# Two attention blocks on one core: A's Exps three tiles behind their projections, other orders at the first transposes and the last out-projections

## The chip, the core and the metric

The kernel runs on one core of a Trainium2 chip. Its engines work side by side, each on its own queue in order: TensorE (PE in the profile, its weight loads PEld) multiplies matrices into PSUM, ScalarE (ACT) computes Exp and copies, VectorE (DVE) does elementwise work and copies, GpSimd (POOL) makes a few constants, SyncE (SP) issues DMAs. An engine waits on semaphores that the others raise. The metric is the device time of one execution in microseconds (us); lower is better. Before the change the median of three runs is 1082.8 us (1082.65 to 1332.74).

## The reference

Two attention blocks work on separate inputs of shape 1 x 2048 x 512, with 32 heads of 16 channels, and their outputs stand side by side in the last dimension.

```python
# A: linear attention                         # B: softmax attention
qkv = x @ wqkv ; q, k, v per head             qkv = x @ wqkv ; q, k, v per head
phi(t) = where(t > 0, t + 1, exp(t)) + 1e-6   p = softmax(q @ k.T * 16 ** -0.5)
pq, pk = phi(q), phi(k)                       o = p @ v
o = (pq @ (pk.T @ v)) / (pq . sum(pk) + 1e-6)
out_a = o @ wo                                out_b = o @ wo
```

## The kernel before

**Block B is the backbone.** Its scores are cut into blocks of 128 keys by 512 queries. A unit is one of two heads in each of four pairs (four heads at once, in four row groups of the array) for one chunk of 512 queries: 64 blocks. There are 32 units, 2048 blocks, and a tile is three blocks, so 683 tiles. For tile s, `QK(s)` (L453) is three matmuls into one of two PSUM buffers pS of three banks each, `EXP(s)` (L462) is one ScalarE Exp over 128 x 1536 from pS into one of NP = 8 SBUF buffers PT, and `PV` (L469) is one matmul a block into pPV, where a unit accumulates. At the end of a unit VectorE copies pPV to OT (L475), and `unit_norm` transposes and divides (L484 to L490).

**The order is written by a loop over steps s.** A step emits what `later` has put at this step, then `EXP(s)`, `QK(s + 2)`, up to six `PV`s of tiles before s, and then at most one misc job (`issue_misc`). QK(s + 2) needs the PSUM buffer that EXP(s) reads. Each engine runs its own instructions in the order in which they were emitted.

**Misc jobs** are all other work: B's remaining projections (`proj`, `vproj`), block A as a whole, norms and out-projections. They share one PSUM bank, MISC (pM). Each job has a hold, the number of steps until the next one may be issued. Block A's are, in order: transposes of x (L356), then for each of 16 row tiles `a_k` (L536, four matmuls of 512 columns, hold 4) and `a_v` (L544, the same size, hold 2), four `a_kv`, then in four rounds four `a_q` (L563, four matmuls of 512 columns, hold 4), a denominator, and four times numerator, transpose (`out_tr`, L501/L504) and out-projection (`out_mm`, L511/L514, four matmuls of 512 columns, then a store to DRAM).

**phi.** `a_k` and `a_q` end in `phi`: ScalarE takes an Exp of pM into EA (L526), VectorE clamps EA (L527) and combines (L529). `later(1, st1)` puts these three one step after the projection, so that in ScalarE's queue EA's Exp stands right ahead of EXP(s + 1). There are 32 of them.

**Start and end.** Ahead of the loop PE warms up with 14 small matmuls (L604), four pairs of row tiles of x are transposed into six borrowed pS banks, and the first projections run. After the loop the last unit's four row tiles go one after the other through out_tr and out_mm in the bank MISC, with VectorE alone copying out. Then `bound_end` (L395 to L403) reduces bounds on the scores to one number FLG. Every engine loads FLG and branches (L737, L738): above a threshold a general, slower softmax would run. With these inputs it does not.

Of the kernel before, what the change touches and what calls it, by code (L numbers as in the profile page):

```python
# [19 lines left out]
class Sched:  # L20
# [75 lines left out]

    def emit_queue(self, queue, eng, sems, dma_inc=16):
        waited = {}
        for op in self.queue_ops[queue]:
            for d in op.waits:  # L100
                is_dma = d.lane not in self.ENGINES
                val = d.count * (dma_inc if is_dma else 1)
                if waited.get(d.lane, 0) >= val:
                    continue
                eng.wait_ge(sems[d.lane], val)
                waited[d.lane] = val
            ins = op.fn(eng)
# [105 lines left out]
def bass_concat_heads__linear_attn_block__softmax_full_mha__prompt_kernel(nc, A_x, A_wqkv, A_wo, B_x, B_wqkv, B_wo, out):  # L213
# [8 lines left out]
    TB = 3  # L222
    NP = 8
    NBLK = NU * NT * 4
# [4 lines left out]
    with es:  # L229
# [24 lines left out]
        ZR = sb("ZR", [128, 2, 16], F32)  # L254
        ONT = sb("ONT", [128, 2, 512], BF)
        OB = sb("OB", [128, 4, 512], BF)
        OA = sb("OA", [128, 2, 512], BF)
# [108 lines left out]
        def proj(bk, Gp, sc, kind, lane="dve"):  # L366
# [8 lines left out]
            if kind == 0:  # L375
                ev("dve", bk, lambda e, bk: e.tensor_copy(QT[:, r, cs], f32v(bk)), [], [("QT", r, sc)])
            else:
                for e_ in range(2):
                    ev("dve", bk, lambda e, bk, e_=e_: e.tensor_scalar(KM[:, r, e_, cs], f32v(bk), PAR[:, e_:e_ + 1], None, op0=ALU.mult),  # L379
                       [("PAR", e_)], [("KM", r, e_, sc)])  # L380
# [113 lines left out]

        out_lanes = {"a": [sch.new_dma_lane() for _ in range(2)], "b": [sch.new_dma_lane() for _ in range(2)]}
        stores = []
# [10 lines left out]
        def out_mm(bk, ab, t, o2, lane="dve"):  # L507
            WO, wkey, col0, o4 = (WOa, "WOa", 0, o2) if ab == "a" else (WOb, "WOb", 512, 2 + o2)
            def mm(e, bk):
                for hb in range(4):  # L510
                    ins = e.matmul(f32v(bk), lhsT=ONT[:, o2, hb * 128:(hb + 1) * 128], rhs=WO[:, hb, :], start=(hb == 0), stop=(hb == 3))  # L511
                return ins
            pe(bk, mm, [("ONT", o2), wkey])
            ev(lane, bk, lambda e, bk: (e.tensor_copy(OB[:, o4, :], f32v(bk)) if lane == "dve"  # L514
                                        else e.activation(OB[:, o4, :], f32v(bk), ACTF.Copy)), [], [("OB", o4)])
            stores.append(sch.add(out_lanes[ab][o2], lambda e: e.dma_start(out[0][t * 128:(t + 1) * 128, col0:col0 + 512], OB[:, o4, :]),
                                  reads=[("OB", o4)], queue="sp", force_signal=True))

# [3 lines left out]
        def phi(bk, out_ap, okeys):  # L522
            q = ectr[0] % 2
            ectr[0] += 1
            def st1():
# [76 lines left out]
        def warm(e):  # L602
            for i_ in range(14):
                ins = e.matmul(MB[:, 0:128], lhsT=identb[:], rhs=identb[:], start=True, stop=True)  # L604
            return ins
        sch.add("pe", warm, reads=["identb"], writes=["MB"])
        xb_in = lambda t: on_keys(t) + on_keys(t + 1)
        xT(SBANKS[0], ON, xb_in(0), xTb, "xTb", 0, lane="dve")
        xT(SBANKS[1], ON, xb_in(2), xTb, "xTb", 2, lane="act")
        proj(SBANKS[2], 0, 0, 1)  # L610
        proj(SBANKS[3], 0, 0, 0)
        xT(SBANKS[4], ON, xb_in(4), xTb, "xTb", 4, lane="act")
        xT(SBANKS[5], ON, xb_in(6), xTb, "xTb", 6, lane="dve")
# [17 lines left out]
        for Gp in range(1, NGP):  # L631
# [4 lines left out]
            for sc in range(NC):  # L636
                for kind in (1, 0):
                    bproj.append((r0, 3, lambda bk, Gp=Gp, sc=sc, kind=kind: (proj(bk, Gp, sc, kind), later(2, lambda: bound(Gp, sc, kind)))))
        aj = []
        for t in range(0, NT, 2):  # L640
            aj.append((0, 2, lambda bk, t=t: xT(bk, KNa, [("KNa", t), ("KNa", t + 1)], xTa, "xTa", t)))
        for t in range(NT):
            aj.append((0, 4, lambda bk, t=t: a_k(bk, t)))
            aj.append((0, 2, lambda bk, t=t: a_v(bk, t)))
        for bq in range(4):
            aj.append((0, 3, lambda bk, bq=bq: a_kv(bk, bq)))
        for sc in range(NC):
            for bq in range(4):
                aj.append((0, 4, lambda bk, sc=sc, bq=bq: a_q(bk, sc, bq)))
            aj.append((0, 3, lambda bk, sc=sc: a_den(bk, sc)))  # L650
# [17 lines left out]
        def unit_done(u, s):  # L668
# [4 lines left out]
            if Gp == NGP - 1 and e_ == 1:  # L673
                for tl in range(4):
                    t = 4 * c + tl
                    outb_q.append((s + 4, 2, lambda bk, t=t: out_tr(bk, ON[:, t, :], on_keys(t), t % 2)))
                    outb_q.append((s + 4, 2, lambda bk, t=t: out_mm(bk, "b", t, t % 2)))

        QK(0)
        QK(1)  # L680
        npv = 0
# [3 lines left out]
        while True:  # L685
# [26 lines left out]
            if s >= NTILE and npv == NBLK and not (norm_q or early or bproj or outb_q or aj) and not at_step:  # L712
                break
        bound_end(MISC)

        last = {}
# [17 lines left out]
        def run(queue, e):  # L734
            sch.emit_queue(queue, e, sems)
            e.wait_ge(sems["dve"], flag_op.count)
            v = e.value_load(FLG.bitcast(mybir.dt.int32)[0:1, 0:1], min_val=0)  # L737
            with e.If(v > THRESHOLD_BITS):  # L738
                for ln, tot in totals.items():
# [52 lines left out]
```

## Time and profile before

The profiled execution took 1080.88 us, its span, from the first to the last instruction, is 1079.2 us.

| | before |
|---|---|
| median of three runs | 1082.8 us |
| profiled execution | 1080.88 us |
| its span | 1079.2 us |
| ScalarE busy | 942.0 us, 87% of the span |
| PE busy | 827.3 us, 77% |
| VectorE busy | 225.4 us, 21% |
| mean granted clock of TensorE | 0.749 of full speed |

ScalarE is busiest. A busy PE need not be at its peak, since matmuls overlap. The granted clock of a stretch is a mean over its two levels, 1.0 (2.4 GHz) and 0.5 (1.2 GHz).

### The profile page before, as it was taken

The numbers are of one execution on the slowest core, as the hardware profiler recorded it, in microseconds if no ns is written. First come the engines' busy times: TensorE is split into PE (matmuls) and PEld (weight loads), VectorE is DVE, ScalarE is ACT, GpSimd is POOL, SyncE is SP. The second block draws the span as 40 slices with busy tenths as digits, with TensorE's granted clock in tenths as the row PEclk, the third lists the DMA queues.
The fourth block names the chain that finished last, engine by engine and source line by source line (L and its number), as shares of the span: only waits on it lengthen the run. The fifth ranks groups of instructions, "written<-read, shape, count | busy, mean of one in ns | idle before, by whom it ended". The sixth has DMA issues, their size and how long they took to land.

```text
span 1079.2 us, 11753 instructions
## 1 busy us (share of the span) xinstructions
PE 827.3 (77%) x5212; PEld 227.0 (21%) x5264; DVE 225.4 (21%) x395; ACT 942.0 (87%) x719; POOL 4.9 (0%) x16
## 2 busy tenths in 40 slices
PE   6877777776777776876886877687888887888875
PEld 3322221111111221221221222122111112121211
DVE  3532431111211331121221234112000002010202
ACT  5999998767877997897887999789999999999990
POOL 1000000000000000000000000000000000000000
PEclk9999997677776996596676689658655558585865
DMA  9000000000000000000000000000000000000000
GB/s 310 2 1 1 1 1 1 0 1 1 1 1 0 1 1 1 1 15 5 5 15 1 5 6 5 6 1 15 5 1 1 1 1 20 1 20 1 16 5 22
DMA packets 13128, 13.39 MB, mean 12 GB/s; under 512 B 1808, under 2 KB 12560, under 8 KB 13072
## 3 DMA queue, kind: packets, MB, share of 16 engines
q1 hardware_dynamic: 12272, 12.19, 3.5%
q8 instruction: 42, 0.69, 0.3%
q10 hardware_dynamic: 800, 0.39, 0.1%
q14 instruction: 14, 0.11, 0.0%
HBM read 8.39 MB, written 4.19 MB: 12 GB/s over the span
## 4 chain that ended last, share of the span: by engine, by line
ACT 73%; PE 23%; DVE 1%; issue 1%; DMA 0%
ACT PT L462 71%; PE pS L453 6%; PE pPV L469 6%; PE pM L544 2%; PE pM L511 2%; PE pM L563 2%; ACT EA L526 2%; PE pM L536 1%; PE pM L484 1%; PE pM L501 1%; DMA ON<-in_B_x_dram 0%; PE pS L369 0%; PE pM L369 0%; PE pS L356 0%; DVE KM L379 0%
## 5 line engine op out<-in xcount | busy, mean ns | idle before, releaser
L462 ACT ACTIVATE PT<-pS 128x1536 bf16<-128x1536 f32 (+1 forms) x683 | 922.6, 1591 | 13.7 <-PE pS L453 12.8
L453 PE MATMUL pS<-QT,KM 32*128 32x512 bf16 x2048 | 338.6, 490 | 219.7 <-ACT PT L462 218.3
L469 PE MATMUL pPV<-PT,VV 128*17 128x512 bf16 x2048 | 333.6, 488 | 1.3 <-DVE VV L426 0.9
L453 PEld LDWEIGHTS pS<-QT,KM 32*128 32x128 bf16 x2048 | 69.0, 95 | 496.3 <-ACT PT L462 473.0
L469 PEld LDWEIGHTS pPV<-PT,VV 128*17 128x17 bf16 x2048 | 62.3, 89 | 214.7 <-issue 210.4
L526 ACT ACTIVATE EA<-pM 128x512 bf16<-128x512 f32 x32 | 19.1, 597 | 89.1 <-PE pM L563 45.8
L475 DVE COPY OT<-pPV 128x512 f32<-128x512 f32 x32 | 22.1, 691 | 236.1 <-PE pPV L469 236.0
L514 DVE CAST OB<-pM 128x512 bf16<-128x512 f32 x32 | 22.1, 692 | 89.5 <-PE pM L511 89.5
L527 DVE TENSOR_SCALAR EA<-EA 128x512 bf16<-128x512 bf16 x32 | 9.4, 294 | 113.9 <-ACT EA L526 113.9
L369 PE MATMUL pM<-xTb,Wb 128*128 128x512 bf16 x108 | 29.2, 390 | 3.3 <-DVE xTb L363 1.7
L547 DVE CAST VNa<-pM 128x512 bf16<-128x512 f32 x16 | 11.1, 694 | 98.7 <-PE pM L544 98.7
L484 PE MATMUL pM<-identf,OT 128*128 128x128 f32 x128 | 29.3, 370 | 1.3 <-DVE OT L475 1.3
L379 DVE TENSOR_SCALAR KM<-pM,PAR 128x512 bf16<-128x512 f32 x30 | 21.1, 746 | 35.5 <-PE pM L369 35.5
L544 PE MATMUL pM<-Wa,xTa 128*128 128x512 bf16 x58 | 26.3, 601 | 1.9 <-issue 1.9
L504 DVE COPY ONT<-pM 128x512 bf16<-128x512 bf16 x32 | 13.6, 425 | 57.7 <-PE pM L501 57.7
L563 PE MATMUL pM<-xTa,Wa 128*128 128x512 bf16 x57 | 22.4, 531 | 1.6 <-issue 1.6
L511 PE MATMUL pM<-WOb,ONT 128*128 128x512 bf16 x57 | 20.4, 490 | 3.8 <-DVE ONT L504 2.5
L488 DVE RECIPROCAL ZR<-pM 128x16 f32<-128x16 f32 x32 | 8.2, 257 | 70.0 <-PE pM L484 70.0
L484 PEld LDWEIGHTS pM<-identf,OT 128*128 128x128 f32 x128 | 18.7, 184 | 15.8 <-issue 7.9
L511 PE MATMUL pM<-WOa,ONT 128*128 128x512 bf16 x50 | 19.6, 496 | 2.7 <-issue 2.6
L390 DVE TENSOR_REDUCE KMX<-KM 128x1 f32<-128x1024 bf16 x16 | 19.5, 1217 | 0.4
L590 DVE TENSOR_TENSOR OA<-pM,RD 128x512 bf16<-128x512 f32 x16 | 11.1, 691 | 25.0 <-PE pM L586 25.0
(76 smaller groups left out, 253.9 us busy)
## 6 DMA issues: line engine op xcount, KB each, us to landing
out_dram<-OB SPq DMA_DIRECT2D x32, 128.0 KB, 1.7
KNa<-in_A_x_dram SPq DMA_DIRECT2D x4, 512.0 KB, 8.3
ON<-in_B_x_dram SPq DMA_DIRECT2D x3, 512.0 KB, 7.7
Wa<-in_A_wqkv_dram SPq DMA_DIRECT2D x1, 1536.0 KB, 12.6
Wb<-in_B_wqkv_dram SPq DMA_DIRECT2D x2, 384.0 KB, 8.4
Wb<-in_B_wqkv_dram SPq DMA_DIRECT2D x1, 512.0 KB, 6.8
WOb<-in_B_wo_dram SPq DMA_DIRECT2D x1, 512.0 KB, 12.7
WOa<-in_A_wo_dram SPq DMA_DIRECT2D x1, 512.0 KB, 12.5
```

The lines of the kernel that those rows point to most:

```text
L369: ins = e.matmul(f32v(bk), lhsT=Wb[:, cc, kind * 512 + Gp * 128:kind * 512 + Gp * 128 + 128], rhs=xTb[:, cc, sc * 512:(sc + 1) * 512], sta ...
L379: ev("dve", bk, lambda e, bk, e_=e_: e.tensor_scalar(KM[:, r, e_, cs], f32v(bk), PAR[:, e_:e_ + 1], None, op0=ALU.mult), [("PAR", e_)], [( ...
L453: ins = e.matmul(SCR[b][:, i * 512:(i + 1) * 512], lhsT=KM[32 * g:32 * g + 32, Gp % 2, e_, j * 128:(j + 1) * 128], rhs=QT[32 * g:32 * g + ...
L462: sch.add("act", lambda e: e.activation(PT[:, t % NP, 0:w], SCR[b][:, 0:w], ACTF.Exp, scale=SC), reads=skeys(b), writes=[("PT", t % NP)], ...
L469: sch.add("pe", lambda e: e.matmul(PVb[32 * g:32 * g + 17, 0:512], lhsT=VV[:, j, 17 * h:17 * h + 17], rhs=PT[:, t % NP, i * 512:(i + 1) * ...
L475: sch.add("dve", lambda e: e.tensor_copy(OT[:, u % 2, :], PVb[:, 0:512]), reads=[("PV", g) for g in range(4)], writes=[("OT", u % 2)])
L484: ins = e.transpose(f32v(bk)[:, qb * 128:(qb + 1) * 128], OT[:, ob, qb * 128:(qb + 1) * 128], identf[:])
L511: ins = e.matmul(f32v(bk), lhsT=ONT[:, o2, hb * 128:(hb + 1) * 128], rhs=WO[:, hb, :], start=(hb == 0), stop=(hb == 3))
L514: ev(lane, bk, lambda e, bk: (e.tensor_copy(OB[:, o4, :], f32v(bk)) if lane == "dve" else e.activation(OB[:, o4, :], f32v(bk), ACTF.Copy)) ...
L526: ev("act", bk, lambda e, bk: e.activation(EA[:, q, :], f32v(bk), ACTF.Exp), [], [("EA", q)])
L544: ins = e.matmul(f32v(bk), lhsT=xTa[:, cc, t * 128:(t + 1) * 128], rhs=Wa[:, cc, 1024:1536], start=(cc == 0), stop=(cc == 3))
L563: ins = e.matmul(f32v(bk), lhsT=Wa[:, cc, bq * 128:(bq + 1) * 128], rhs=xTa[:, cc, sc * 512:(sc + 1) * 512], start=(cc == 0), stop=(cc == 3))
```

## The change

The Exps of phi move from one step after the projection to three, and `a_k` and `a_q` hold MISC for five steps, not four. The first transposes take one row tile each, copied out alternately by VectorE and ScalarE; QK(0) and QK(1) come earlier, and two transposes and a projection behind them; the warm-up is 28 matmuls, not 14. When all tiles are through, the last four transposes and then the last four out-projections go over the six pS banks, copied out alternately by ScalarE and VectorE, with more ONT and OB buffers and six store lanes. `bound_end` becomes a misc job behind B's last projection; a hook has each engine load FLG in mid-queue, so that only the branch stays at the end. NP becomes 7.

```diff
@@ emit_queue
+            if hook is not None and op.idx > hook[0]:
+                hook[1](eng)
+                hook = None
             ins = op.fn(eng)
@@
-    NP = 8
+    NP = 7
@@
-        ONT = sb("ONT", [128, 2, 512], BF)
-        OB = sb("OB", [128, 4, 512], BF)
+        ONT = sb("ONT", [128, 6, 512], BF)
+        OB = sb("OB", [128, 6, 512], BF)
@@ proj
             if kind == 0:
-                ev("dve", bk, lambda e, bk: e.tensor_copy(QT[:, r, cs], f32v(bk)), [], [("QT", r, sc)])
+                ev(lane, bk, lambda e, bk: (e.tensor_copy(QT[:, r, cs], f32v(bk)) if lane == "dve"
+                                            else e.activation(QT[:, r, cs], f32v(bk), ACTF.Copy)), [], [("QT", r, sc)])
@@ phi
-            later(1, st1)
+            later(3, st1)
@@ the start
-            for i_ in range(14):
+            for i_ in range(28):
...
-        xT(SBANKS[0], ON, xb_in(0), xTb, "xTb", 0, lane="dve")
-        xT(SBANKS[1], ON, xb_in(2), xTb, "xTb", 2, lane="act")
-        proj(SBANKS[2], 0, 0, 1)
-        proj(SBANKS[3], 0, 0, 0)
-        xT(SBANKS[4], ON, xb_in(4), xTb, "xTb", 4, lane="act")
-        xT(SBANKS[5], ON, xb_in(6), xTb, "xTb", 6, lane="dve")
+        for t in range(4):
+            xT(SBANKS[t], ON, on_keys(t), xTb, "xTb", t, n=1, lane=("dve", "act")[t % 2])
+        proj(SBANKS[4], 0, 0, 1)
+        proj(SBANKS[5], 0, 0, 0, lane="act")
+        QK(0)
+        xT(MISC, ON, xb_in(4), xTb, "xTb", 4, lane="dve")
+        QK(1)
+        xT(MISC, ON, xb_in(6), xTb, "xTb", 6, lane="dve")
         proj(MISC, 0, 1, 1)
@@ the misc lists
+        bproj.append((0, 2, bound_end))
...
-            aj.append((0, 4, lambda bk, t=t: a_k(bk, t)))
+            aj.append((0, 5, lambda bk, t=t: a_k(bk, t)))
...
-                aj.append((0, 4, lambda bk, sc=sc, bq=bq: a_q(bk, sc, bq)))
+                aj.append((0, 5, lambda bk, sc=sc, bq=bq: a_q(bk, sc, bq)))
@@ issue_misc
+            if s > NTILE and not (norm_q or bproj or early):
+                tail[0] = True
+                if outb_q:
+                    jobs = outb_q[0::2] + outb_q[1::2]
+                    outb_q.clear()
+                    for _, _, fn in jobs:
+                        fn(SBANKS[tail[1] % 6])
+                        tail[1] += 1
+                    return
@@ the end
-        bound_end(MISC)
...
-            sch.emit_queue(queue, e, sems)
-            e.wait_ge(sems["dve"], flag_op.count)
-            v = e.value_load(FLG.bitcast(mybir.dt.int32)[0:1, 0:1], min_val=0)
-            with e.If(v > THRESHOLD_BITS):
+            got = []
+            def hook(e):
+                e.wait_ge(sems["dve"], flag_op.count)
+                got.append(e.value_load(FLG.bitcast(mybir.dt.int32)[0:1, 0:1], min_val=0))
+            sch.emit_queue(queue, e, sems, hook=(flag_op.idx + 200, hook))
+            with e.If(got[0] > THRESHOLD_BITS):
```

Three places show what moves. The first is ScalarE's queue where block A's `a_k` jobs begin; PT rows are tiles' Exps, EA rows are phi's. Before:

```order
L462 ACTIVATE PT<-pS 128x1536 x103
L526 ACTIVATE EA<-pM 128x512
L462 ACTIVATE PT<-pS 128x1536 x8
L526 ACTIVATE EA<-pM 128x512
L462 ACTIVATE PT<-pS 128x1536 x6
```

And of the change, at the same place:

```order
L468 ACTIVATE PT<-pS 128x1536 x105
L532 ACTIVATE EA<-pM 128x512
L468 ACTIVATE PT<-pS 128x1536 x9
L532 ACTIVATE EA<-pM 128x512
L468 ACTIVATE PT<-pS 128x1536 x7
```

The first EA has moved behind two more tiles, while its projection stands on PE where it stood; from one EA to the next there are seven tiles, where there were six (nine for eight where a norm comes between).

The second place is PE's queue from its first matmul on. Before:

```order
L604 MATMUL pM<-identb 128x128 x14
L356 MATMUL pS<-identb,ON 128x128 x16
L369 MATMUL pS<-xTb,Wb 128x512 x8
L356 MATMUL pS<-identb,ON 128x128 x16
L369 MATMUL pM<-xTb,Wb 128x512 x4
L453 MATMUL pS<-QT,KM 128x512 x9
```

And of the change:

```order
L610 MATMUL pM<-identb 128x128 x28
L361 MATMUL pS<-identb,ON 128x128 x16
L374 MATMUL pS<-xTb,Wb 128x512 x8
L459 MATMUL pS<-QT,KM 128x512 x3
L361 MATMUL pM<-identb,ON 128x128 x8
L459 MATMUL pS<-QT,KM 128x512 x3
L361 MATMUL pM<-identb,ON 128x128 x8
L374 MATMUL pM<-xTb,Wb 128x512 x4
```

QK(0) now stands right behind the first two projections; the second half of the transposes and the third projection stand between QK(0) and QK(2).

The third place is the end of PE's queue, from the last unit's transposes on (identf, OT). Before:

```order
L484 MATMUL pM<-identf,OT 128x128 x4
L501 MATMUL pM<-identb,ON 128x128 x4
L511 MATMUL pM<-WOb,ONT 128x512 x4
...
L402 MATMUL pM<-BMk,BN 1x128
L737 TENSOR_LOAD FLG
L737 REGISTER_ALU
L737 ISA
L738 COMPARE_AND_BRANCH
```

And of the change:

```order
L490 MATMUL pM<-identf,OT 128x128 x4
L507 MATMUL pS<-identb,ON 128x128 x16
L517 MATMUL pS<-WOb,ONT 128x512 x16
L762 COMPARE_AND_BRANCH
```

Four alternations of transpose and out-projection in pM have become all transposes and then all out-projections in pS, and the work for FLG and its load are gone from the end.

## Rows read from the trace of the kernel before

**Rows 1.** The page: shares of the chain that ended last, by engine.

```profile
ACT 73%; PE 23%; DVE 1%; issue 1%; DMA 0%
```

**Rows 2.** Groups by line: shapes, count | busy us, mean ns | idle before, releasers.

```profile
L462 ACT ACTIVATE PT<-pS 128x1536 bf16<-128x1536 f32 (+1 forms) x683 | 922.6, 1591 | 13.7 <-PE pS L453 12.8 <-PE pPV L469 0.6
L526 ACT ACTIVATE EA<-pM 128x512 bf16<-128x512 f32 x32 | 19.1, 597 | 89.1 <-PE pM L563 45.8 <-PE pM L536 43.3
```

**Rows 3.** ScalarE's timeline: start us, us, engine, line [idle before <-releaser].

```profile
156.47 0.60 ACT L526 ACTIVATE EA<-pM 128x512 bf16<-128x512 f32 x1 [1.77 <-PE pM L536]
...
353.53 53.84 ACT L462 ACTIVATE PT<-pS 128x1536 bf16<-128x1536 f32 x40 [0.74 <-PE pS L453]
...
418.16 0.60 ACT L526 ACTIVATE EA<-pM 128x512 bf16<-128x512 f32 x1 [3.05 <-PE pM L563]
...
458.01 26.97 ACT L462 ACTIVATE PT<-pS 128x1536 bf16<-128x1536 f32 x20 [0.92 <-PE pS L453]
...
1008.88 45.38 ACT L462 ACTIVATE PT<-pS 128x1536 bf16<-128x1536 f32 x34 [0.94 <-PE pS L453]
```

**Rows 4.** Timeline around one a_v and the a_k behind it.

```profile
184.76 5.50 ACT L462 ACTIVATE PT<-pS 128x1536 bf16<-128x1536 f32 x4
...
187.62 0.61 PE L453 MATMUL pS<-QT,KM 32*128 32x512 bf16 x3 [0.20 <-ACT PT L462]
...
189.10 1.49 PE L544 MATMUL pM<-Wa,xTa 128*128 128x512 bf16 x3 [0.33 <-issue]
...
190.52 0.61 PE L453 MATMUL pS<-QT,KM 32*128 32x512 bf16 x3
...
191.59 0.61 PE L453 MATMUL pS<-QT,KM 32*128 32x512 bf16 x3
...
193.76 0.60 ACT L526 ACTIVATE EA<-pM 128x512 bf16<-128x512 f32 x1 [3.50 <-PE pM L536]
194.25 8.16 ACT L462 ACTIVATE PT<-pS 128x1536 bf16<-128x1536 f32 x6
```

**Rows 5.** PE's timeline around one four-matmul projection in another stage.

```profile
372.49 0.39 PE L453 MATMUL pS<-QT,KM 32*128 32x512 bf16 x3 [0.63 <-ACT PT L462]
...
373.14 1.04 PE L369 MATMUL pM<-xTb,Wb 128*128 128x512 bf16 x4
374.11 0.39 PE L453 MATMUL pS<-QT,KM 32*128 32x512 bf16 x3
```

**Rows 6.** Stretches: busy us (count) of PE, PEld, DVE, ACT, POOL, clock, DMA.

```profile
155.00:354.00 199.00, 144.15 (x775) 35.50 (x784) 33.70 (x63) 152.92 (x123) 0.00 (x0) 0.73 0.00 1
354.00:408.00 54.00, 40.36 (x347) 14.53 (x347) 20.08 (x34) 53.37 (x40) 0.00 (x0) 1.00 0.00 1
408.00:458.00 50.00, 37.40 (x204) 9.11 (x204) 8.22 (x16) 38.65 (x31) 0.00 (x0) 0.60 0.00 1
760.00:800.00 40.00, 33.29 (x184) 7.21 (x184) 2.75 (x6) 40.00 (x31) 0.00 (x0) 0.58 0.01 3
```

**Rows 7.** Timeline of the start.

```profile
6.48 1.02 ACT L363 ACTIVATE xTb<-pS 128x1024 bf16<-128x1024 bf16 x1 [3.13 <-PE pS L356]
...
7.56 3.60 PE L369 MATMUL pS<-xTb,Wb 128*128 128x512 bf16 x8 [1.12 <-ACT xTb L363]
...
33.64 2.79 ACT L462 ACTIVATE PT<-pS 128x1536 bf16<-128x1536 f32 x2 [0.63 <-PE pPV L469]
```

**Rows 8.** Timeline of the end.

```profile
1057.62 0.61 PE L501 MATMUL pM<-identb,ON 128*128 128x128 bf16 x4 [0.81 <-DVE ON L490]
...
1062.55 1.89 PE L511 MATMUL pM<-WOb,ONT 128*128 128x512 bf16 x4 [0.52 <-DVE ONT L504]
...
1072.07 0.69 DVE L514 CAST OB<-pM 128x512 bf16<-128x512 f32 x1 [1.98 <-PE pM L511]
...
1073.98 0.28 DVE L403 TENSOR_REDUCE FLG<-pM 1x1 f32<-1x128 f32 x1 [0.68 <-PE pM L402]
```

**Rows 9.** Waits of SP's queue: waited for: us in total, times, longest.

```profile
SPq L229 <- PEq L229: 3.7, 1, 3.7
```

**Rows 10.** PE's timeline around one end of a unit.

```profile
881.75 0.60 PE L469 MATMUL pPV<-PT,VV 128*17 128x512 bf16 x2
...
884.73 1.03 PE L469 MATMUL pPV<-PT,VV 128*17 128x512 bf16 x6
...
886.23 0.61 PE L469 MATMUL pPV<-PT,VV 128*17 128x512 bf16 x4
```

More of the change, by code (lines that the diff above doesn't have):

```diff
@@ L95, in finalize, with emit_queue @@
                     o.count = c
-    def emit_queue(self, queue, eng, sems, dma_inc=16):
+    def emit_queue(self, queue, eng, sems, dma_inc=16, hook=None):
         waited = {}
@@ L110, in emit_queue @@
                 ins.then_inc(sems[op.lane], dma_inc if is_dma else 1)
+        if hook is not None:
+            hook[1](eng)
 THRESHOLD_BITS = 0x42700000
@@ L493, in unit_norm @@
                 op=ALU.mult), [("ZR", ob)], [("ON", t, 2 * Gp + e_) for t in range(4 * c, 4 * c + 4)])
-        out_lanes = {"a": [sch.new_dma_lane() for _ in range(2)], "b": [sch.new_dma_lane() for _ in range(2)]}
+        out_lanes = [sch.new_dma_lane() for _ in range(6)]
         stores = []
@@ L507, in out_mm @@
         def out_mm(bk, ab, t, o2, lane="dve"):
-            WO, wkey, col0, o4 = (WOa, "WOa", 0, o2) if ab == "a" else (WOb, "WOb", 512, 2 + o2)
+            WO, wkey, col0 = (WOa, "WOa", 0) if ab == "a" else (WOb, "WOb", 512)
             def mm(e, bk):
@@ L513, in out_mm @@
             pe(bk, mm, [("ONT", o2), wkey])
[L514 to L517, printed above, removed]
+            ev(lane, bk, lambda e, bk: (e.tensor_copy(OB[:, o2, :], f32v(bk)) if lane == "dve"
+                                        else e.activation(OB[:, o2, :], f32v(bk), ACTF.Copy)), [], [("OB", o2)])
+            stores.append(sch.add(out_lanes[o2], lambda e: e.dma_start(out[0][t * 128:(t + 1) * 128, col0:col0 + 512], OB[:, o2, :]),
+                                  reads=[("OB", o2)], queue="sp", force_signal=True))
         ectr = [0]
@@ L656, in bass_concat_heads__linear_attn_block__softmax_full_mha__prompt_kernel, with ev_lane @@
         free_at = [0]
+        tail = [False, 0, 0]
+        def ev_lane():
+            if not tail[0]:
+                return "dve"
+            tail[2] += 1
+            return ("act", "dve")[tail[2] % 2]
         def issue_misc(s):
@@ L675, in unit_done @@
                     t = 4 * c + tl
[L676 to L680, printed above, removed]
+                    outb_q.append((s + 4, 2, lambda bk, t=t: out_tr(bk, ON[:, t, :], on_keys(t), 2 + t % 4, ev_lane())))
+                    outb_q.append((s + 4, 2, lambda bk, t=t: out_mm(bk, "b", t, 2 + t % 4, ev_lane())))
         npv = 0
```

## The prediction

> **What bounds the kernel now.** I read the chain of waits on the page first: nearly three quarters of what ended last is ScalarE [rows 1]. The groups by line then say what ScalarE does and what it waits for. Its 683 tile Exps have only 13.7 us of idle time before them; its 32 Exps of phi have 89.1 us, 45.8 behind `a_q` and 43.3 behind `a_k` [rows 2]. ScalarE's timeline gives the pace when nothing is in the way: 40 tiles in 53.84 us, 1.345 us a tile [rows 3]. From an EA to the tile behind it is 0.49 us (193.76 to 194.25) [rows 4]. So 682 full tiles, a last one of about 0.9 and 32 EAs need 918 + 16 = 934 us of a span of 1079.2. The other 145 us are waits, the start and the end.
>
> **Why EA waits.** Follow one step. When EXP(s) is done, PE starts QK(s + 2), the PVs and then the projection, but EA's Exp stands in ScalarE's queue right ahead of EXP(s + 1), so ScalarE stands still until the projection is done, though EXP(s + 1) has its scores. The wait takes two usual sizes: 1.77 us and 3.05 us [rows 3], or more where an `a_v` shortly before has put PE behind: 3.50 in the pair shown [rows 4]. The two sizes are PE's two clocks. From one QK to the next with four matmuls of 512 columns between them is 2.90 us at the low clock (187.62 to 190.52) [rows 4] and 1.62 us at the full one (372.49 to 374.11) [rows 5].
>
> **Part 1, EA three tiles later.** ScalarE now has EXP(s + 1) and EXP(s + 2), 2 x 1.345 = 2.69 us, between the start of the projection's step and EA. I compare that with PE from the same moment.
> At the full clock QK(s + 3) ends 1.62 + 0.39 = 2.01 us after QK(s + 2) began [rows 5], before ScalarE wants anything: nothing waits.
> At the low clock the projection ends 189.10 + 1.49 - 187.62 = 2.97 us in and QK(s + 3) 2.90 + 0.61 = 3.51 us in [rows 4]. EA is wanted at 2.69 and EXP(s + 3) at 2.69 + 0.49 = 3.18, so about 0.3 to 0.4 us is lost. I take 0.4.
> A job of the same size without an EA (`a_v`, an out-projection) loses 3.51 - 2.69 = 0.8 at the low clock; that stall is there before, 0.92 and 0.94 ahead of a tile's Exp [rows 3].
> An `a_v` and the `a_k` two tiles behind it, both low, need 2.90 + 1.07 + 2.90 + 0.61 = 7.5 us of PE (1.07 is a tile without a job, 190.52 to 191.59 [rows 4]). ScalarE has four tiles and an EA for it, 5.38 + 0.49 = 5.9: 1.6 us lost.
>
> *Removed:* the 89.1 us of EA waits and four of the waits ahead of tiles in the stretch of the `a_k` jobs, 0.56 to 0.92, together 2.9 (0.74 is one [rows 3]), which are the same PE backlog. 92.0 in all.
>
> *Coming back:* sixteen `a_k`/`a_v` pairs at 0 to 1.6 us each, 0 to 26. Which clock will they have? This stretch has 0.73 now, with ScalarE standing still and PE running dry behind it. The stretch of 354 to 408, with a four-matmul job every third tile and ScalarE never waiting, has 1.00; with no such jobs at all the clock is 0.58 [rows 6]. Two jobs in seven tiles is nearly one in three, so I take a value nearer to the full clock, 0.5 us a pair: 8. Sixteen `a_q` come alone, one in five tiles where it was one in four, and that stretch has 0.60 [rows 6], so I take fourteen at the low clock: 14 x 0.4 = 5.6, between 0 and 6.4. The other nine waits ahead of tiles (0.57 to 0.94, first and last shown [rows 3], together 7.7) stay.
>
> The longer holds cost nothing in themselves: 32 jobs push the misc list back by 32 steps, and in ScalarE's queue of the change 214 tiles still stand behind the last EA. What EA releases on VectorE (clamp, combine, and with them the bank pM) has the rest of the five held steps, two tiles, to be done in.
>
> On TensorE's clock the row comes first: a stretch in which PE always had something queued kept 1.00, and the one with gaps fell to 0.73 [rows 6]. The Trainium skill, "TensorE: Matmul & The Clock Gate" (section "What's actually happening"), says that the throttled level is the default and that activity releases it. By that rule alone, with the gaps gone, the pairs would lose nothing and the sum would be 8 us lower; the row with 0.58, where PE is 83% busy at the low clock, says that it need not.
>
> **Part 2, the start.** Before, the 14th tile starts at 33.64, behind a PV, since all eight PT buffers are taken [rows 7]. With seven the 13th tile meets that wait: one tile, +1.35 us, if PE's chain of transposes, projections and VectorE copies up to that PV is no earlier. It can be earlier: half-size copies save some 0.4 of 1.02, and the first eight matmuls, 3.60 us at the low clock, take 1.8 less if the longer warm-up has raised it [rows 7]. That is -2.2 + 1.35 = -0.9. QK(0) is earlier by far, but QK(2) now stands behind a projection that ran ahead of it, so ScalarE only waits elsewhere. I take 0, between -0.9 and +1.35.
>
> **Part 3, the flag.** `bound_end` goes to mid-run, a few short VectorE operations and a small matmul, under ScalarE's tiles. The load of FLG in mid-queue is nowhere in the rows as an instruction. After FLG (1073.98 + 0.28 [rows 8]) the span has 4.9 us left, of which SP waits 3.7 for PE's queue [rows 9]; load and end barrier share the remaining 1.2. So an engine is held at most 1.2 us, at least 0, since a tile's Exp of 1.345 covers it. I take 0.6.
>
> **Part 4, the end.** From the first transpose at 1057.62 to the last copy at 1072.07 + 0.69 = 1072.76 is 15.1 us, in which PE and VectorE take turns [rows 8]. Over free banks PE goes through: 4 x 0.61 + 4 x 1.89 + one copy of 0.69 = 10.7 at the low clock, 4.4 less. The first of the out-projections waits for a copy of the first transpose, which is done while the others run. The 1.5 us from the last copy to FLG go, and up to 0.6 of the load. Together 6.5. If the clock rises in ten dense microseconds, up to half of 7.56 more. And the branch on PE can begin before the last copy. I take -8, between -5.5 and -10.5. The 3.7 us of the branch stay: the Trainium skill, "Runtime: NRT & Kernel Launch" (section "Instruction fetch mechanics"), says that a taken branch out of the fetched window waits for a fetch. The trace agrees: 3.7 [rows 9].
>
> **Sum.** -92.0 + 8 + 5.6 + 0 + 0.6 - 8 = -85.8. The span of 1079.2 becomes 993.4, the profiled 1080.88 becomes 995.1, and the median, which is 1.9 above the profiled time, becomes 1082.8 - 85.8 = 997.
>
> **The rivals.**
> *The clock stays up.* With ScalarE running through, PE is fed evenly and its clock stays at 1.0 through block A. Then the 8 and the 5.6 vanish, the nine remaining waits of 7.7 too, and the end gives 2.5 more: 997 - 24 = 973. For it speaks the stretch of 354 to 408; against it the 0.58 where no misc work runs [rows 6].
> *The clock stays down.* All pairs lose 1.6 (26, not 8), all `a_q` 0.4 (6.4), and all 28 out-projections inside the loop 0.92 (25.8, where 7.7 stand now): 997 + 18 + 0.8 + 18 = 1034. The move then does less than it says, since PE is the bound in these stretches. For it speaks 0.60 in 408 to 458; against it, that a PE that is the bound has no gaps, and the low clock was seen with gaps.
> *The ring of seven binds at every unit's end.* PVs pause there: 881.75 to 884.73, 3.0 us, and then 6 + 4 blocks are made up, a backlog of about three tiles [rows 10]. If the backlog filled the ring, ScalarE would wait out the pause 32 times: 32 x 3.0 = 95, and 997 + 95 = 1092, slower than before. It decides from 85.8 / 32 = 2.7 us a unit on, for which PVs would have to lag seven tiles, not three. Nothing in the rows shows that outside the start [rows 7].
>
> **How the numbers follow.** The forecast, between 985 and 1010, gets 0.55; the clock up, 960 to 985, 0.23; the clock down, 1010 to 1045, 0.18; the ring 0.02; something else that takes the gain 0.02. A range from 973 to 1018 leaves out about half of the clock-up case and half of the clock-down case, 0.2. A difference of 2% is about what a measurement of this kernel can tell; 2% faster is 1061, which all cases but the ring lie below. Faster 0.96, within 2% 0.02, slower 0.02.
>
> **What would show it.** Right: in the profile after, the EA group has a few us of idle time, not 89; ScalarE is busy for about 94% of the span; waits ahead of tiles, 13.7 before, grow to 15 to 25; the last out-projections take about 10 us from their first transpose; FLG's reduction stands in the middle. The granted clock in the `a_k` stretch tells the first two rivals apart: 0.9 or more, or 0.6 and less. The start is right if the chain to the tile that waits for a PV ends within 1.5 us of where it did. Wrong: many waits of tiles' Exps on pPV (the ring), or EA waits of 1 us and more (PE three tiles behind).

## The result: 997.6 us, ratio 0.922, and the profile after

The changed kernel takes 997.63 us (median of 4 runs, 995.05 to 999.74) against 1082.72 us for the kernel before: a ratio of 0.9217, 95% interval 0.9188 to 0.9246. One of the four runs of the kernel before, at 1332.74 us, was in a slow state, and the ratio leaves it out. The forecast was 997 us, between 973 and 1018. The profiled execution of after has a span of 995.6 us.

The page of after first: span, busy times, the clock in 40 slices, the chain of waits by engine.

```profile
span 995.6 us, 11777 instructions
PE 776.1 (78%) x5219; PEld 227.0 (23%) x5278; DVE 222.9 (22%) x392; ACT 944.3 (95%) x724; POOL 4.9 (0%) x16
PEclk9999999788788989779679798687785569596776
ACT 77%; PE 20%; DVE 1%; issue 1%; POOL 0%; POOLq 0%
```

ScalarE is now busy for 95% of the span; its busy time is nearly what it was (942.0 before). So the 83.6 us that the span lost were idle time of ScalarE. The groups by line say which (busy us, mean ns | idle us ahead of the group and what ended it):

```profile
L468 ACT ACTIVATE PT<-pS 128x1536 bf16<-128x1536 f32 (+1 forms) x683 | 926.7, 1603 | 28.9 <-PE pS L459 26.4 <-PE pPV L475 2.3
L532 ACT ACTIVATE EA<-pM 128x512 bf16<-128x512 f32 x32 | 20.9, 654 | 3.8 <-PE pM L569 3.2 <-PE pM L542 0.6
```

Against [rows 2], the Exps of phi wait 3.8 us instead of 89.1. The tiles wait 28.9 us instead of 13.7, nearly all of it for scores. ScalarE's list of waits (us in total, times, longest) says where the seven buffers bind: two waits on pPV in the whole execution.

```profile
ACT PT L468 <- PE pS L459: 26.4, 35, 1.3
ACT PT L468 <- PE pPV L475: 2.3, 2, 1.8
```

**Where the time went.** I cut the span at the 18th tile, by which the start is over, and at the end of the last tile's Exp.

| us | before | after | difference | forecast |
|---|---|---|---|---|
| up to the 18th tile | 39.1 | 41.1 | +2.0 | 0 |
| 18th tile to the last Exp's end | 1015.2 | 940.1 | -75.1 | -77.8 |
| from there to the span's end | 24.9 | 14.4 | -10.5 | -8 |
| span | 1079.2 | 995.6 | -83.6 | -85.8 |

**The middle.** The same pair as in [rows 4], `a_v` (L550) and then `a_k` (L542), now looks like this on PE and ScalarE:

```profile
177.59 0.61 PE L459 MATMUL pS<-QT,KM 32*128 32x512 bf16 x3 [0.63 <-ACT PT L468]
...
178.67 1.89 PE L550 MATMUL pM<-Wa,xTa 128*128 128x512 bf16 x4
...
180.49 0.61 PE L459 MATMUL pS<-QT,KM 32*128 32x512 bf16 x3
...
181.15 2.79 ACT L468 ACTIVATE PT<-pS 128x1536 bf16<-128x1536 f32 x2 [0.92 <-PE pS L459]
...
182.22 0.81 PE L542 MATMUL pM<-Wa,xTa 128*128 128x512 bf16 x3 [0.16 <-issue]
...
183.82 0.61 ACT L532 ACTIVATE EA<-pM 128x512 bf16<-128x512 f32 x1
184.30 4.16 ACT L468 ACTIVATE PT<-pS 128x1536 bf16<-128x1536 f32 x3
```

EA comes without a wait, since its projection was done long before. What is left is the 0.92 us behind the `a_v`, which runs at the low clock: 2.90 us from QK to QK (177.59 to 180.49). The `a_k` behind it already runs at the full clock, so this pair loses 0.92 us, not 1.6.

ScalarE's waits by stretch, tiles and EA together, from its lists of waits: 7.9 + 0.6 us where the `a_k` run (158 to 332), against 2.9 + 43.3 before; 12.0 + 3.2 us from 359 to 745, where the `a_q` and most out-projections run, against 3.3 + 45.8 (the 0.74 ahead of 353.53 [rows 3] is in the 2.9); and 0.9 us from there to the end, against 4.4. The clock in these stretches (busy us and count of PE, PEld, DVE, ACT, POOL; clock; DMA):

```profile
158.00:332.00 174.00, 130.89 (x828) 35.96 (x840) 35.52 (x65) 165.30 (x132) 0.00 (x0) 0.83 0.00 1
332.00:359.00 27.00, 20.36 (x151) 6.11 (x151) 13.40 (x18) 26.69 (x21) 0.00 (x0) 1.00 0.00 1
...
399.00:443.00 44.00, 35.41 (x219) 9.27 (x221) 7.99 (x16) 42.42 (x34) 0.00 (x0) 0.70 0.00 1
745.00:800.00 55.00, 45.98 (x257) 9.52 (x254) 2.75 (x6) 55.00 (x42) 0.00 (x0) 0.56 0.00 1
```

The `a_k` stretch has 0.83, where it had 0.73 [rows 6], the first `a_q` 0.70 (0.60 before), and 0.56 stands where no misc job runs, as before (0.58).

**The start.** ScalarE's timeline of after, against [rows 7]:

```profile
10.26 2.79 ACT L468 ACTIVATE PT<-pS 128x1536 bf16<-128x1536 f32 x2 [0.49 <-PE pS L459]
14.37 1.45 ACT L468 ACTIVATE PT<-pS 128x1536 bf16<-128x1536 f32 x1 [1.31 <-PE pS L459]
...
24.22 6.82 ACT L468 ACTIVATE PT<-pS 128x1536 bf16<-128x1536 f32 x5 [0.54 <-PE pPV L475]
32.81 4.14 ACT L468 ACTIVATE PT<-pS 128x1536 bf16<-128x1536 f32 x3 [1.77 <-PE pPV L475]
38.08 2.79 ACT L468 ACTIVATE PT<-pS 128x1536 bf16<-128x1536 f32 x2 [1.13 <-PE pS L459]
41.11 4.13 ACT L468 ACTIVATE PT<-pS 128x1536 bf16<-128x1536 f32 x3 [0.24 <-PE pS L459]
```

The first tile starts at 10.26, 4.4 us earlier than before (14.63), and all of that is given back by the 13th. The eighth tile, the first to want a used one of the seven buffers, and the thirteenth wait for a PV, 2.3 us in sum. Behind the 13th (32.81) two more waits follow, for scores: 1.13 us ahead of the 16th tile and 0.24 ahead of the 18th (41.11).

**The end**, PE's and ScalarE's timeline against [rows 8]:

```profile
984.54 1.89 PE L507 MATMUL pS<-identb,ON 128*128 128x128 bf16 x16 [0.81 <-DVE ON L496]
...
986.65 5.04 PE L517 MATMUL pS<-WOb,ONT 128*128 128x512 bf16 x15 [0.22 <-DVE ONT L510]
...
989.21 0.15 PEld L517 LDWEIGHTS pS<-WOb,ONT 128*128 128x128 bf16 x1 [0.28 <-issue]
989.64 0.15 PEld L517 LDWEIGHTS pS<-WOb,ONT 128*128 128x128 bf16 x1 [0.28 <-issue]
...
990.02 1.18 PEld L517 LDWEIGHTS pS<-WOb,ONT 128*128 128x128 bf16 x6 [0.23 <-issue]
...
991.73 0.60 ACT L521 ACTIVATE OB<-pS 128x512 bf16<-128x512 f32 x1 [1.25 <-PE pS L517]
```

From the first transpose to the last copy's end (991.73 + 0.60) it is 7.8 us instead of 15.1. The weight loads are 0.43 us apart up to 989.64 and then six come in 1.18 us, so PE went to the full clock about 990. After the last copy the span has 3.3 us left, where it had 6.4.

Why it is 3.3 the branches show. PE's row before, and then of after PE's and GpSimd's branch and GpSimd's load of FLG (duration in ns min/median/max, first and last start in us; PEld is PE's own queue):

```profile
L738 PEldq COMPARE_BRANCH  x1: 3748/3748/3748, 1075.1 to 1075.1; - x1
```

```profile
L762 PEldq COMPARE_BRANCH  x1: 3328/3328/3328, 987.1 to 987.1; - x1
...
L762 POOLq COMPARE_BRANCH  x1: 45/45/45, 995.1 to 995.1; - x1
```

```profile
L760 POOLq TENSOR_LOAD <-FLG x1: 477/477/477, 994.5 to 994.5; - x1
```

Before, PE came to its branch behind the load of FLG and held the span's end for 3.75 us. Now it comes to it at 987.1, while its last matmuls run to 991.69, and is through with both by 991.7. What stands last is GpSimd: it waits for the last store to land, and only then loads FLG, from 994.5 on, and branches. GpSimd has no work in mid-run, and the wait for the stores is the next entry of its queue, so the hook comes there: for this engine the load of FLG still stands at the end.

### The profile page after: what moved, and what is told of

It is laid out like the page before. It is cut to its first block, busy times and chain, and to the rows that moved or that the text cites. A ratio compares the mean times of both kernels' runs of the same rounds, so it can differ in the third digit from the quotient of the medians.

```text
span 995.6 us, 11777 instructions
## 1 busy us (share of the span) xinstructions
PE 776.1 (78%) x5219; PEld 227.0 (23%) x5278; DVE 222.9 (22%) x392; ACT 944.3 (95%) x724; POOL 4.9 (0%) x16
## 4 chain that ended last, share of the span: by engine, by line
ACT 77%; PE 20%; DVE 1%; issue 1%; POOL 0%; POOLq 0%
ACT PT L468 76%; PE pS L459 6%; PE pPV L475 5%; ACT EA L532 2%; PE pM L550 2%; PE pM L517 1%; PE pM L569 1%; PE pM L490 1%; PE pM L374 1%; PE pS L517 1%; PE pM L428 1%; DVE KM L385 0%; DVE xTb L368 0%; PE pM L361 0%; PE pM L610 0%
## 5 line engine op out<-in xcount | busy, mean ns | idle before, releaser
L468 ACT ACTIVATE PT<-pS 128x1536 bf16<-128x1536 f32 (+1 forms) x683 | 926.7, 1603 | 28.9 <-PE pS L459 26.4
L459 PE MATMUL pS<-QT,KM 32*128 32x512 bf16 x2048 | 317.6, 459 | 192.2 <-ACT PT L468 190.1
L475 PE MATMUL pPV<-PT,VV 128*17 128x512 bf16 x2048 | 314.1, 459 | 1.3 <-DVE VV L432 0.9
L520 DVE CAST OB<-pM 128x512 bf16<-128x512 f32 x28 | 19.4, 692 | 84.1 <-PE pM L517 79.7
L550 PE MATMUL pM<-Wa,xTa 128*128 128x512 bf16 x53 | 21.2, 534 | 2.8 <-issue 2.8
L542 PE MATMUL pM<-Wa,xTa 128*128 128x512 bf16 x58 | 16.5, 405 | 1.1 <-issue 1.1
```

Source lines behind the costliest of these rows:

```text
L459: ins = e.matmul(SCR[b][:, i * 512:(i + 1) * 512], lhsT=KM[32 * g:32 * g + 32, Gp % 2, e_, j * 128:(j + 1) * 128], rhs=QT[32 * g:32 * g + ...
L468: sch.add("act", lambda e: e.activation(PT[:, t % NP, 0:w], SCR[b][:, 0:w], ACTF.Exp, scale=SC), reads=skeys(b), writes=[("PT", t % NP)], ...
L475: sch.add("pe", lambda e: e.matmul(PVb[32 * g:32 * g + 17, 0:512], lhsT=VV[:, j, 17 * h:17 * h + 17], rhs=PT[:, t % NP, i * 512:(i + 1) * ...
L550: ins = e.matmul(f32v(bk), lhsT=xTa[:, cc, t * 128:(t + 1) * 128], rhs=Wa[:, cc, 1024:1536], start=(cc == 0), stop=(cc == 3))
```

## The experiments

Each is timed beside the kernel before on the same chip (its medians there were 1082.7 to 1083.5 us).

| kernel | median us | lowest to highest | ratio to before, 95% interval |
|---|---|---|---|
| Exps alone | 1007.06 | 1006.05 to 1014.96 | 0.9303 [0.9279, 0.9328] |
| Exps undone | 1074.53 | 1073.33 to 1074.72 | 0.9916 [0.9891, 0.9940] |
| start undone | 999.23 | 995.13 to 1001.16 | 0.9231 [0.9211, 0.9251] |
| eight buffers | 999.61 | 996.96 to 1001.89 | 0.9237 [0.9216, 0.9258] |
| end serial | 1006.10 | 1004.25 to 1012.12 | 0.9307 [0.9270, 0.9345] |
| two steps | 1036.82 | 1034.61 to 1038.77 | 0.9571 [0.9545, 0.9596] |
| QK twice | 1000.46 | 992.32 to 1005.23 | 0.9216 [0.9167, 0.9265] |
| spread | 1002.67 | 998.19 to 1010.48 | 0.9270 [0.9234, 0.9307] |
| spread, eight buffers | 1004.00 | 1002.94 to 1010.56 | 0.9279 [0.9255, 0.9303] |
| the same, old start | 1004.67 | 1003.67 to 1008.60 | 0.9280 [0.9262, 0.9298] |
| fill 256 | 1044.62 | 1040.80 to 1051.09 | 0.9664 [0.9636, 0.9692] |
| fill 384 | 1070.41 | 1063.16 to 1077.49 | 0.9872 [0.9841, 0.9903] |

### The Exps alone, and everything but them

Into the kernel before:

```diff
-            later(1, st1)
+            later(3, st1)
...
-            aj.append((0, 4, lambda bk, t=t: a_k(bk, t)))
+            aj.append((0, 5, lambda bk, t=t: a_k(bk, t)))
...
-                aj.append((0, 4, lambda bk, sc=sc, bq=bq: a_q(bk, sc, bq)))
+                aj.append((0, 5, lambda bk, sc=sc, bq=bq: a_q(bk, sc, bq)))
```

> The kernel before with the first part alone: phi's Exps three steps behind, a_k and a_q holding the bank for five; start, end, flag and the eight buffers as before. If EA's place is nearly the whole gain, the stretch from the 18th tile to the last Exp falls by the 75 us that the two traces differ by there, and the time by as much: 1082.7 - 75 = 1007. If the other parts carry a good share (an earlier first Exp, a raised clock, freer engines), it stays at 1030 or above.

The second kernel is after with these three lines put back.

> The changed kernel with the first part undone (Exps one step behind, hold four). If the parts add up, start and end alone give +2 and -10.5 us: 1074. If the end's gain needs ScalarE to arrive as it does in the changed kernel, or the start and the end are worth more, it is below 1065; if they are worth nothing alone, 1083.

Alone the Exps take 76.2 us off, everything else 8.7; together 84.9, and the whole change took 85.1. Each of the two is known to within about 2.7 us (its interval), so that they meet to 0.2 is luck. The groups of EA, first with the Exps alone, then with them undone:

```profile
L526 ACT ACTIVATE EA<-pM 128x512 bf16<-128x512 f32 x32 | 20.8, 649 | 4.4 <-PE pM L563 4.3
```

```profile
L532 ACT ACTIVATE EA<-pM 128x512 bf16<-128x512 f32 x32 | 19.1, 597 | 90.0 <-PE pM L569 46.7 <-PE pM L542 43.2
```

The 89 us come and go with these three lines, and with nothing else of the change. The hold moves with EA's place here; the next kernel moves EA alone.

### Two steps instead of three

```diff
-            later(3, st1)
+            later(2, st1)
```

The hold stays at five.

> The changed kernel with phi's Exps two steps behind, not three. From the start of QK(s+2) ScalarE has one tile, 1.345 us, before EA. The projection ends 1.69 us in at the full clock and 2.97 at the low one, so an EA loses 0.35 or 1.6: with half of 32 at each, 31 us of EA waits for 3.8 now, and fewer waits ahead of tiles: 1015 to 1030. If one more tile was all that was needed, EA waits stay under 8 us and the time under 1003.

It lost 39 us, more than the 17 to 32 expected. EA's group has 32.8 us of idle time, about what was expected, in the expected two sizes. ScalarE's timeline of this kernel:

```profile
160.77 0.60 ACT L532 ACTIVATE EA<-pM 128x512 bf16<-128x512 f32 x1 [0.43 <-PE pM L542]
...
187.43 0.60 ACT L532 ACTIVATE EA<-pM 128x512 bf16<-128x512 f32 x1 [1.65 <-PE pM L542]
```

What I missed is that the waits ahead of tiles do not shrink in exchange: 38.3 us against 28.9. The EA waits follow the arithmetic of part 1: a projection that is done 2.97 us in at the low clock, less one tile of 1.345 us, leaves 1.6; with two tiles, 2.69 us, it leaves 0.3. And since the hold is the same in both kernels, it is EA's place that moves them.

### The start undone, and eight buffers

The start undone is after with the old order: four pairs of row tiles, 14 warm-up matmuls, QK(0) and QK(1) last.

> The changed kernel with the old start (pairs of row tiles, 14 warm-up matmuls, QK(0) and QK(1) behind the first projections). In the changed kernel the first Exp starts 4.4 us earlier, but the 18th tile 2.1 us later than before. If a chain of PE and VectorE and the seven buffers bind there, the old start with seven buffers has its 13th tile where the 14th stood, 33.6, so the 18th at 40.4, and the time is 997 within 1 us. If the earlier first Exp is a gain, the time rises by up to 4.4, to 1002.

Eight buffers makes room for the eighth by smaller output buffers:

```diff
-    NP = 7
+    NP = 8
...
-        ONT = sb("ONT", [128, 6, 512], BF)
-        OB = sb("OB", [128, 6, 512], BF)
+        ONT = sb("ONT", [128, 4, 512], BF)
+        OB = sb("OB", [128, 4, 512], BF)
...
-                    outb_q.append((s + 4, 2, lambda bk, t=t: out_mm(bk, "b", t, 2 + t % 4, ev_lane())))
+                    outb_q.append((s + 4, 2, lambda bk, t=t: out_mm(bk, "b", t, t % 4, ev_lane())))
```

> The changed kernel with eight PT buffers (and four ONT and OB buffers, not six, to make room). If the ring binds only at the start, one tile is won there, 1.3 us, and part of a second wait of 1.1 us behind it: 995 to 997, and no wait on pPV later. If seven buffers bind elsewhere too, the waits ahead of tiles outside the start, 21.7 us now, fall, and the time with them, to 985 or so.

Neither moves the time: 1.6 and 2.0 us above after, inside the runs' spread of 5 to 6 us. In the traces the ring shows. The start with eight buffers and the new order:

```profile
28.15 2.79 ACT L468 ACTIVATE PT<-pS 128x1536 bf16<-128x1536 f32 x2 [0.37 <-PE pS L459]
31.57 31.06 ACT L468 ACTIVATE PT<-pS 128x1536 bf16<-128x1536 f32 x23 [0.63 <-PE pPV L475]
```

One wait of 0.63 for a PV, as before the change, and then 23 tiles without a stop. With the old order and seven buffers the waits for PVs are 0.41 and 1.77 us. The difference of the two sums, 1.7 us (2.3 - 0.6), is not yet the ring's price: a tile that does not wait for a PV may wait for its scores instead. The two spread kernels below differ in their buffers and begin alike (first tile at 9.74 and 9.68 us, clock 0.66 from 12 to 37 us in both): with seven the 13th tile stands behind a PV at 36.06, with eight the 14th at 35.99, and the 18th comes 1.5 us earlier. That is the one tile of the prediction:

```profile
36.06 24.40 ACT L468 ACTIVATE PT<-pS 128x1536 bf16<-128x1536 f32 x18 [1.97 <-PE pPV L475]
```

```profile
35.99 24.34 ACT L468 ACTIVATE PT<-pS 128x1536 bf16<-128x1536 f32 x18 [0.63 <-PE pPV L475]
```

Over all profiled executions the 18th tile starts between 39.6 and 43.4 us with seven buffers and between 37.0 and 42.8 with eight, whichever order the start has: an execution's own scatter is as large as either effect. It goes roughly with TensorE's clock from 12 to 37 us: with the new start and seven buffers the 18th tile stands at 39.6 where that clock is 0.93, at 41.1 in after with 0.88, and at 41.6 to 43.4 with 0.66 to 0.77.

### The end one tile after the other

```diff
-            if s > NTILE and not (norm_q or bproj or early):
+            if False:
```

> The changed kernel with the last out-projections one after the other in the bank pM, VectorE alone copying out, as before the change; the flag stays in mid-run. In the traces the stretch from the first of these transposes to the last copy fell from 15.1 to 7.8 us, and from the last copy to the end of the span from 6.4 to 3.3. If the free banks bring the first of these and the flag's place the second, the time is 997.6 + 7.3 = 1005. If the flag and the branch bring all of it, it is 999 or less; if the free banks bring all of it, 1008.

8.5 us are lost. The end of this kernel's timeline:

```profile
985.72 0.61 PE L507 MATMUL pM<-identb,ON 128*128 128x128 bf16 x4 [0.81 <-DVE ON L496]
...
998.25 1.89 PE L517 MATMUL pM<-WOb,ONT 128*128 128x512 bf16 x4 [0.52 <-DVE ONT L510]
...
1000.17 0.69 DVE L520 CAST OB<-pM 128x512 bf16<-128x512 f32 x1 [1.98 <-PE pM L517]
```

The 15.1 us are back (985.72 to 1000.86), so the free banks are worth 7.3 of the end's 10.5 us; the early flag keeps its 3: 2.9 us from the last copy to the span's end at 1003.8, where before had 6.4. PE's branch, 3.71 us long here, begins at 998.2, beside the last matmuls, and GpSimd's load of FLG at 1002.7.

### Can the waits that are left be had?

After still waits 25 us outside the start, and in the raw trace the waits stand where PE is at the low clock (in the 3 us before it PE has at most 0.5 us at the full clock, for 23 of 29 waits ahead of tiles and all 10 ahead of EAs). The theory: with more for PE to do the clock rises and the waits go. The rival: the extra work costs as much as it gives.

**QK twice.** The three score matmuls are issued twice from step 120 on, in steps without a misc job right before:

```diff
-                QK(s + 2)
+                QK(s + 2, 2 if s >= 120 and s - last_misc[0] > 1 else 1)
```

> The changed kernel, where from step 120 on QK's three matmuls are issued twice in each step that has no misc job right before it (the second writes the same values over the first). It adds PE work and nothing else. If the waits that are left (21 us ahead of tiles outside the start, 4 ahead of EA) are the low clock, this keeps PE busy enough for the full one, which then shows 0.95 or more in the stretches of a_k and a_q, the waits fall to a few us, and the time to about 977. If they are the length of the jobs themselves, or PE becomes the bound, the time is 998 or more.

The median did not move. The clock did, to a mean of 0.896 from 0.808, in the profiled execution, which is the slowest of four: they go from 1005.2 us at 0.896 to 992.3 at 0.924, less time with more clock. Windows of the profiled one:

```profile
160.00:325.00 165.00, 132.97 (x969) 33.86 (x984) 30.97 (x59) 155.16 (x124) 0.00 (x0) 0.88 0.00 1
394.00:436.00 42.00, 31.51 (x301) 9.10 (x301) 6.83 (x15) 42.00 (x36) 0.00 (x0) 0.99 0.00 1
```

From 394 to 436, with the `a_q`, the clock is 0.99 and ScalarE is busy for all 42 us: where the clock stays up, nothing waits. But in the `a_k` stretch 0.88 still leaves low spells, and there a wait can be longer with the doubled scores:

```profile
219.16 2.95 ACT L468 ACTIVATE PT<-pS 128x1536 bf16<-128x1536 f32 x2 [1.44 <-PE pS L459]
```

1.44 us behind an `a_v`, where after has 0.92.

**Fill.** One more matmul of 256 (or 384) columns in one row group, a repetition of part of the tile's last block, at the end of each QK from tile 120 on:

```diff
+                if t >= 120:
+                    ins = e.matmul(SCR[b][:, i * 512:i * 512 + 256], lhsT=KM[...], rhs=QT[...], start=True, stop=True, tile_position=(32 * g, 0))
```

> The changed kernel with one more small matmul at the end of each QK from tile 120 on: 256 columns of its last block again, the same values over the same place. It adds about 0.11 us of PE work a tile at the full clock and 0.21 at the low one, so that even a low tile, 1.07 + 0.21 = 1.28 us, stays under ScalarE's 1.345. If more activity keeps TensorE's clock up between the jobs, the clock rises from 0.81 to 0.9 or more, the 25 us of waits fall below 15, and the time to 985. If it takes more than that, or the low spells that remain cost more, the time is 995 or above.

> The same with 384 columns: 0.16 us a tile at the full clock, 0.32 at the low one, 1.07 + 0.32 = 1.39 us, a little over ScalarE's pace. If activity decides, the clock is higher than with 256 columns, 0.95, and the time 980 to 985; if the low spells decide, each costs more and the time is 1000 or above.

Both were far off, 1044.6 and 1070.4 us: the mean clock fell, to 0.765 and 0.744. A window of the 256-column kernel where no misc job runs:

```profile
780.00:840.00 60.00, 60.00 (x319) 11.33 (x316) 2.75 (x6) 59.08 (x45) 0.00 (x0) 0.50 0.00 1
```

PE is busy for all 60 us, at the low clock throughout. The Trainium skill, "TensorE: Matmul & The Clock Gate" (section "What's actually happening"), says that activity releases the throttle. This window shows that PE's busy time in a profile cannot be taken for that activity. What in the filler matters was not tried.

**Spread.** `a_v` and the out-projections inside the loop issue one matmul a step instead of four at once (hold 4):

```diff
+        def spread(bk, part, reads, tag, done):
+            def go(k):
+                sch.add("pe", lambda e: part(e, bk, k), reads=reads, writes=[bk[3]], accum=tag)
+                if k == 3:
+                    done()
+            go(0)
+            for k in range(1, 4):
+                later(k + 1, lambda k=k: go(k))
```

> The changed kernel, where a_v and the out-projections inside the loop issue their four matmuls one per step, not all in one, and hold the bank for four steps. The same work, thinner. If the waits ahead of tiles are ScalarE overtaking a four-matmul job at the low clock, a tile with one of these matmuls costs PE 1.07 + 0.45 = 1.52 us there; after four of them QK's scores are due at 6.1 + 0.6 = 6.7 us, when ScalarE, with the two tiles in hand, wants them (5 x 1.345 = 6.7): the 21 us of these waits fall below 8 and the time to 985. If a thinner load only lets the clock fall further, the granted clock drops under 0.75 and the time stays at 995 or more.

Not faster, 5 us slower if anything, and not by a lower clock: it is 0.795, above the rival's 0.75. The 0.92 us stops are gone, but in their place stand small ones, and EA waits 9.0 us, not 3.8. In sum tiles and EAs wait 32.3 us, against 32.7 in after. ScalarE's timeline:

```profile
303.49 1.45 ACT L468 ACTIVATE PT<-pS 128x1536 bf16<-128x1536 f32 x1 [0.16 <-PE pS L459]
305.10 1.45 ACT L468 ACTIVATE PT<-pS 128x1536 bf16<-128x1536 f32 x1 [0.16 <-PE pS L459]
306.72 1.45 ACT L468 ACTIVATE PT<-pS 128x1536 bf16<-128x1536 f32 x1 [0.16 <-PE pS L459]
309.06 0.60 ACT L548 ACTIVATE EA<-pM 128x512 bf16<-128x512 f32 x1 [0.89 <-PE pM L558]
```

At the low clock a tile with one such matmul takes 1.62 us from start to start, more than ScalarE's 1.345. So the backlog that a bunched `a_v` leaves is PE's work itself, and in smaller pieces it costs about the same. The last two kernels add eight buffers, and then the old start, to the spread. In these two A's and B's out-projections meet in the smaller output buffers, so that some rows of the output are another tile's; work and order are otherwise the same.

> The run before (a_v and out-projections one matmul a step) with eight PT buffers, and four ONT and OB buffers. If seven buffers cost at the start what the first runs suggest, the 18th tile starts at 37 to 39 us, not 41 to 43, and the time is 2 to 5 us under that of seven buffers. If TensorE's clock there decides alone, the 18th tile lies anywhere between 37 and 43, and the medians agree within 2 us.

> The run before with the old start as well (pairs of row tiles, 14 warm-up matmuls, QK(0) and QK(1) last). If the new start is a gain once the ring has eight buffers, this has its 18th tile 2 us or more behind the run before, at 39 to 43, and is slower by that; if the start is bound by the chain of projections in either order, both agree within 2 us.

Within 2 us of the spread alone and of each other: the ring and the order of the start do not show here either. No kernel here beats the changed one, and whether its last 25 us can be had stays open.

## Why the prediction was right, step by step

**EA's wait: right.** The removed 92.0 us rested on EA standing ahead of a tile that had its scores. The Exps alone and undone show it: 4.4 and 90.0 us of EA waits.

**The pairs: right in size, by a clock between the rivals'.** I took 8 us, 0.5 for every pair. The `a_k` stretch has 7.9 + 0.6, in ten waits ahead of tiles of up to 0.9 and two of 0.3 ahead of EAs, so some pairs lose more than 0.5 and others nothing. Its clock is 0.83, below the 0.9 that would have told for "the clock stays up" and far above the 0.6 for "the clock stays down". The pair shown is one case of that: an `a_v` at the low clock and its `a_k` at the full one. "PE always had something queued" was a wrong reading of the row with 1.00, since PE is busy for 40.36 of 54 us there; what sets the clock stays open.

**`a_q` and the out-projections: mis-sized.** I took 5.6 us for the `a_q` and left the out-projections inside the loop at what they had, 3.3 us, 8.9 in all. From 359 to 745 the waits are 12.0 + 3.2 = 15.2. The `a_q` themselves are right or a little high: EA waits 3.2 us in 8 waits of 0.4, the size that I took, in half as many jobs. The tiles are off: 12.0 in 16 waits instead of 3.3 in 4, and with them all tiles' waits came to 28.9, above the 15 to 25 that I had named as a sign. I read it so: before, PE caught up on its low-clock backlog while ScalarE stood at an EA; now ScalarE does not pause. No run isolates that. After 745 it went the other way, 0.9 us for 4.4 before, where I had kept them. Together the middle gave 75.1 us where 77.8 were forecast, 6.3 too much waiting in one stretch and 3.5 too little in the other.

**The start: outside its bounds.** I gave 0, between -0.9 and +1.35; it was +2.0. The ring's one tile is right, as the two spread kernels show. The 13th tile stands at 32.81, 0.8 us ahead of the 14th before (33.64), so by my own sign for the start, within 1.5 us, it was right as well. The step that failed is that behind this tile nothing would wait: the two waits for scores, 1.13 and 0.24 us, put the 18th tile at 41.1. The clock from 12 to 37 us is 0.88 in after and 0.93 before. Where it is 0.93 with the same start (fill 384, whose filler begins later) these waits are not there and the 18th tile stands at 39.6, +0.6, inside my bounds:

```profile
32.81 20.37 ACT L472 ACTIVATE PT<-pS 128x1536 bf16<-128x1536 f32 x15 [1.77 <-PE pPV L479]
```

So the rest goes with the clock, which I had not put into this part; whether the new order lowers it or the execution happened on it stays open. The gains of the half-size copies and the early QK(0) were real at the first tile, -4.4 us, and gone at the 13th.

**The flag: not to be seen.** I gave it 0.6 us. The reduction now stands at 611.4 us, and ScalarE loads FLG at 655.7, in the middle of twelve tiles that run without a stop (GpSimd alone loads it at the end):

```profile
644.33 16.23 ACT L468 ACTIVATE PT<-pS 128x1536 bf16<-128x1536 f32 x12 [0.92 <-PE pS L459]
```

**The end: right in direction, at its far bound.** -10.5 against -8. The 10.7 us that I worked out at the low clock took 7.8: the sixteen out-projection matmuls ran without a break, in 5.0 us instead of four times 1.89, with the clock up from about 990 on, and the sixteen transposes took 1.9 instead of four times 0.61. "The 3.7 us of the branch stay" is the step that failed: the branch is still 3.3 us long on PE, but it runs beside the matmuls, and what follows the last copy is its store and GpSimd's load of FLG. I had named an earlier branch as a possibility and not put it into the sum.

**Luck in the total.** The span came 2.2 us above the forecast 993.4, from +2.0 at the start, +2.7 in the middle and -2.5 at the end; that the median lies within 1 us of 997 owes something to these signs.

**The rivals.** The ring at each unit's end is refuted: two waits on pPV, both in the start. The clock stayed neither up nor down; the QK-twice window at 0.99 shows that the first rival's mechanism was right where its condition holds.

## What to carry to other kernels

In an in-order queue, an instruction that waits for another engine's fresh result stalls everything behind it: put it behind as much ready work as that result takes at its slowest, here two tiles, 2.69 us, against 2.97 us of PE at the low clock, which leaves 3.8 us of waits; with one tile 33 us are left. Count the backlog that the producer keeps afterwards, since a stall that goes at one place can partly come back at another (17 of 92 us here), as I read it because its idle time used to be a pause for somebody else. To find what such an edit is worth, run it alone and run all but it: here the two halves added up within the noise of some 4 us. And follow every engine's queue to the end: a load that one engine still has there stands last.

## What I had not expected of the hardware

PE can be busy for 60 of 60 us and be granted the low clock throughout (0.50, the 256-column filler), while doubling matmuls that run in three row groups brought the mean clock from 0.808 to 0.896. More work on PE raised the clock in the one case and lowered it in the other.

The branch at the end took 3.3 to 4.2 us on PE in the fourteen kernels, and 0.05 to 0.07 on the other engines in before and after. PE can be in it while its matmuls still run (987.1 to 990.4, with matmuls up to 991.69), and there it costs nothing. I had cited for it the stall for a fetch behind a taken branch, from the Trainium skill, "Runtime: NRT & Kernel Launch" (section "Instruction fetch mechanics"). The length agrees with a stall on PE; that it is a fetch no run here shows.
